# One reciprocal and one addition per pair of heads in an attention and two-expert kernel

## The chip, the cores and the metric

The kernel runs on one NeuronCore of a Trainium2 chip. The metric is the device time of one launch in microseconds. The engines are called TensorE (PE in the profile, its weight loads PEld), VectorE (DVE), ScalarE (ACT), POOL (GpSimd) and SyncE (SP); each takes its own instructions in order and waits for the others at semaphores.

## The reference

Inputs are q, k and v of shape 2 x 12 x 448 x 64 (batch, heads, positions, width) and two pairs of weights (768 x 2048 and 2048 x 768), all float32.

```python
scores = scale * np.matmul(q, k.transpose(0, 1, 3, 2))
scores = np.where(mask, -1000000000.0, scores)          # causal
scores = scores - np.max(scores, axis=-1, keepdims=True)
attn = np.exp(scores)
attn = attn / (np.sum(attn, axis=-1, keepdims=True) + 1e-09)
x = np.matmul(attn, v)                                  # then (896, 768)
h = x @ w_in                                            # first expert layer
x = (h * np.clip(h + 3.0, 0.0, 6.0) / 6.0) @ w_out
h = x @ w_in2                                           # second: P, Q from h, h^2, h^3
out = (P / (Q + 1e-06)) @ w_out2
```

The sum over a row of `attn` is what the change is about: `1e-09` is added to it, the reciprocal is taken, and the row is multiplied by that.

## The kernel before, in words

Attention goes by pairs of heads: `n` = 0 to 11 is one of six pairs of heads in one of two batches. The 448 positions are cut into seven chunks of 64. A chunk `r` of queries of both heads lies in 128 partitions (64 for each head) and sees (r + 1) x 64 keys, so the seven rows of a pair are 64, 128, ... 448 wide. For each pair there are these steps:

- `scores` (L633, TensorE, two steps), into banks of PSUM.
- `max` (L647, VectorE): adds the mask, writes the row to a tile `e`, and its maximum to the column of that row in a small tile `stat`. A row's tile has two buffers (`EB`), so pair n + 2 writes where pair n was.
- `exp` (L654, ScalarE): in place, with the row's sum as a second result (a short instruction that reads the accumulator follows each).
- `bias` (`a_bias`, L666): adds 1e-9 to the sums, on POOL for pairs 1 to 9, else on ScalarE or VectorE. `reciprocal` (`a_recip`, L670): on VectorE. Both are done twice in a pair: once for the columns of the straight rows 6, 5 and 0 (448, 384 and 64 wide), once for those of the swapped rows 4, 3, 2 and 1 (320, 256, 192 and 128 wide).
- `norm` (`a_norm`, L678): multiplies a row by its reciprocal, seven times in a pair. POOL does it for pairs 1 to 9; for pairs 0, 10 and 11 VectorE and ScalarE may, too.
- `transpose` (L686, TensorE): 14 small transposes for the straight rows, 14 for the swapped ones, each group into two banks.
- `move` (L508, L510): those four banks into SBUF, by ScalarE or VectorE.
- `apply` (L708, TensorE): times v; `x hi` and `x rest` split the result into two parts (L508 and L720).

The order is not written by hand. Every step is added with its cost, the engines that may do it and a due time, and `Program.order` plays the engines in a model of time: again and again it takes, of the steps that can begin, the one that can begin earliest; steps that lie within `LOOK` of an engine's earliest count as equally early, and of these the one with the lowest due time is taken. `AVERSE` is a charge in us on a step for an engine, `STAY` one on the due time where TensorE would change its tiling mode (scores, transposes, apply and the products have different ones). The due time is the pair's time plus entries of `DUE`, `SHIFT`, `HURRY` and `FINE`. The order that results is what each engine's queue gets; on the chip, semaphores alone decide when an instruction begins. Loads of q, k and v are DMAs issued by SyncE, among the weights' loads.

The two expert stages are products (`product`, L940): 2304 matmuls with three passes for each tile of weights and batch. Weights come in chunks of three tiles, in float64, and are split into two float32 parts by ScalarE and VectorE (`top` L846, `join` L851, `w hi` L508, `w rest` L869). The first products may begin, pair by pair, once all scores are done, so that they stand among the last pairs' transposes and applies.

Of the kernel before, what the change touches and what calls it, by code (L numbers as in the profile page):

```python
# [21 lines left out]
NCH = 7  # L22
# [19 lines left out]
class Program:  # L42
# [15 lines left out]

    TILING = {"scores": "quarters", "transpose": "rows", "apply": "columns"}
    DRAIN = 0.16  # L60
    STAY = 142.07
    LOOK = {"act": 0.025, "dma": 0.000, "dve": 0.061, "pe": 0.143, "pool": 0.000}
    UNTIL = 90.0
    AVERSE = {("bias", "act"): 23.796, ("bias", "dve"): 0.010, ("move", "act"): 0.010, ("move", "dve"): 0.028, ("norm", "act"): 9.289, ("w hi", "act"): 0.220, ("w hi", "pool"): 0.908}

    def __init__(self, rings, banks, due):
        self.rings, self.banks, self.due = rings, banks, due
# [159 lines left out]
def c_mm(n, passes):  # L227
# [2 lines left out]


DUE = {
    "load": 641.06,
    "keep": 0.00,
    "fetch": -20.00,
    "load v": 986.54,
    "norm": 605.40,
    "scores": -621.59,
    "max": 453.18,
    "exp": 669.50,  # L240
    "bias": -555.36,
    "reciprocal": -3821.56,
    "transpose": -2284.96,
    "move": -1862.28,
    "apply": -251.47,
    "x hi": -335.61,
    "x rest": -1522.19,
    "constants": 166.20,
    "w load": 1207.86,
    "top": 1391.57,  # L250
    "join": 4152.81,
    "w hi": 3197.25,
    "w rest": 1692.49,
    "product": 0.00,
    "relu": -472.26,
    "gate": -35.40,
# [18 lines left out]
    "store": 7.50,  # L275
}
PAIR = 5.5
SHIFT = {0: -402.17, 1: 59.39, 2: -1243.06, 3: -600.07, 4: -53.66, 5: -852.91, 6: -483.55, 7: -206.83, 8: -52.38, 9: 238.94, 10: 591.04, 11: 134.07}

HURRY = {0: 1406.07, 1: -2185.22, 2: -1459.89, 3: -470.07, 4: -843.76, 5: -462.43, 6: 966.12, 7: -966.25, 8: -1410.93, 9: 889.14, 10: -1126.45, 11: -161.36}  # L280
FINE = {
    ("apply", 0): -900.09,
    ("apply", 1): -361.68,
    ("apply", 2): 713.65,
    ("apply", 3): -51.47,
    ("apply", 4): 56.64,
    ("apply", 5): -605.77,
    ("apply", 6): -213.06,
    ("apply", 7): -760.02,
    ("apply", 8): 961.00,  # L290
    ("apply", 9): -43.05,
    ("apply", 10): 335.21,
    ("apply", 11): -376.05,
    ("bias", 0): 226.99,
    ("bias", 1): -289.77,
    ("bias", 2): -1211.59,
    ("bias", 3): -661.92,
    ("bias", 4): 137.09,
    ("bias", 5): 909.85,
    ("bias", 6): -84.77,  # L300
    ("bias", 7): 31.83,
    ("bias", 8): 194.45,
    ("bias", 9): -548.16,
    ("bias", 10): 1678.18,
    ("bias", 11): 960.60,
    ("exp", 0): -272.24,
    ("exp", 1): 296.63,
    ("exp", 2): 1968.38,
    ("exp", 3): 135.65,
    ("exp", 4): 1497.08,  # L310
    ("exp", 5): -310.31,
    ("exp", 6): -1124.12,
    ("exp", 7): 123.92,
    ("exp", 8): -625.90,
    ("exp", 9): -93.28,
    ("exp", 10): -1001.23,
    ("exp", 11): 388.45,
    ("load", 0): -1063.61,
    ("load", 1): -1277.69,
    ("load", 2): 140.13,  # L320
    ("load", 3): 251.36,
    ("load", 4): 146.42,
    ("load", 5): -37.97,
    ("load", 6): 782.51,
    ("load", 7): -328.43,
    ("load", 8): 554.29,
    ("load", 9): -193.50,
    ("load", 10): -67.48,
    ("load", 11): 512.54,
    ("load v", 0): -77.97,  # L330
    ("load v", 1): 587.48,
    ("load v", 2): 124.45,
    ("load v", 3): 878.92,
    ("load v", 4): -626.75,
    ("load v", 5): -695.84,
    ("load v", 6): 341.59,
    ("load v", 7): 545.32,
    ("load v", 8): 832.41,
    ("load v", 9): -802.78,
    ("load v", 10): 327.34,  # L340
    ("load v", 11): -114.21,
    ("max", 0): 162.46,
    ("max", 1): 780.96,
    ("max", 2): 324.74,
    ("max", 3): 559.50,
    ("max", 4): 694.16,
    ("max", 5): -572.65,
    ("max", 6): 553.74,
    ("max", 7): 296.32,
    ("max", 8): -353.83,  # L350
    ("max", 9): -428.08,
    ("max", 10): 1388.07,
    ("max", 11): 403.46,
    ("move", 0): 1230.75,
    ("move", 1): 1212.60,
    ("move", 2): -1400.97,
    ("move", 3): 1123.55,
    ("move", 4): 8.69,
    ("move", 5): 686.35,
    ("move", 6): -202.87,  # L360
    ("move", 7): 296.53,
    ("move", 8): 881.18,
    ("move", 9): 1710.46,
    ("move", 10): 172.45,
    ("move", 11): -165.14,
    ("norm", 0): 402.44,
    ("norm", 1): -274.51,
    ("norm", 2): -1317.40,
    ("norm", 3): 1224.05,
    ("norm", 4): -405.04,  # L370
    ("norm", 5): -119.22,
    ("norm", 6): -950.02,
    ("norm", 7): -460.55,
    ("norm", 8): -406.99,
    ("norm", 9): 532.31,
    ("norm", 10): 985.93,
    ("norm", 11): 850.79,
    ("reciprocal", 0): 132.61,
    ("reciprocal", 1): -682.70,
    ("reciprocal", 2): 476.82,  # L380
    ("reciprocal", 3): -497.26,
    ("reciprocal", 4): 215.96,
    ("reciprocal", 5): -308.28,
    ("reciprocal", 6): 510.69,
    ("reciprocal", 7): -798.76,
    ("reciprocal", 8): -500.60,
    ("reciprocal", 9): 254.09,
    ("reciprocal", 10): 427.19,
    ("reciprocal", 11): -262.09,
    ("scores", 0): 1319.98,  # L390
    ("scores", 1): 44.03,
    ("scores", 2): -675.00,
    ("scores", 3): 317.05,
    ("scores", 4): 1376.15,
    ("scores", 5): 741.99,
    ("scores", 6): 436.50,
    ("scores", 7): 701.37,
    ("scores", 8): -1737.51,
    ("scores", 9): -134.48,
    ("scores", 10): 606.54,  # L400
    ("scores", 11): -305.58,
    ("transpose", 0): -673.78,
    ("transpose", 1): -1595.48,
    ("transpose", 2): -282.36,
    ("transpose", 3): -614.95,
    ("transpose", 4): -257.88,
    ("transpose", 5): -1165.44,
    ("transpose", 6): -235.67,
    ("transpose", 7): -1067.59,
    ("transpose", 8): 344.74,  # L410
    ("transpose", 9): -54.30,
    ("transpose", 10): 521.17,
    ("transpose", 11): -740.95,
    ("x hi", 0): -623.98,
    ("x hi", 1): -1662.06,
    ("x hi", 2): 73.95,
    ("x hi", 3): -1809.87,
    ("x hi", 4): -10.52,
    ("x hi", 5): 376.53,
    ("x hi", 6): 8.43,  # L420
    ("x hi", 7): 16.98,
    ("x hi", 8): 357.94,
    ("x hi", 9): -975.33,
    ("x hi", 10): 98.15,
    ("x hi", 11): -867.64,
    ("x rest", 0): -707.65,
    ("x rest", 1): 396.94,
    ("x rest", 2): 1345.13,
    ("x rest", 3): 838.55,
    ("x rest", 4): 400.60,  # L430
    ("x rest", 5): 291.33,
    ("x rest", 6): 419.34,
    ("x rest", 7): -416.87,
    ("x rest", 8): -292.29,
    ("x rest", 9): -598.63,
    ("x rest", 10): -252.52,
    ("x rest", 11): -615.30,
}


# [18 lines left out]
def tile_attention_moe_moe2(  # L459
# [134 lines left out]
    STRAIGHT, SWAPPED = (6, 5, 0), (4, 3, 2, 1)  # L594
# [44 lines left out]
    LINEUP = [r for held in (STRAIGHT, SWAPPED) for r in held]  # L639
# [16 lines left out]
            accum_out=stat[:, 1, at_:at_ + 1],  # L656
        )

    PARTS = slice(0, len(STRAIGHT)), slice(len(STRAIGHT), NCH)

    def a_bias(e, n, part):
        stat, c = tiles["stat", n], PARTS[part]
# [62 lines left out]
    def put(kind, at, *what, **uses):  # L725
        add(kind, at + FINE.get((kind, n), 0.0), *what, **uses)

    for n in range(len(pairs)):
        t, last = PAIR * n + SHIFT.get(n, 0.0), n == len(pairs) - 1
        b, hp = pairs[n]  # L730
        for which in ("kr", "qr"):

            group, whole = (which, "all", hp), hp > 1
            if whole and b:
                continue
            for parts in ((0,), (1,)) if n == 0 else ((0, 1),):
# [5 lines left out]
                    writes=[(which, x, j) for x in range(n, n + (B if whole else 1)) for j in parts],  # L742
                    new=[(which, group)] if b == 0 and 0 in parts else (),
                )
        if b == 0:
            put(
                "load v", t, {"dma": 4.3}, v_load, hp, reads=[("empty", hp % VB)],
                writes=[("v", hp), ("turn", "v")], new=[("v", ("v", hp))],
            )
        for step in range(2):  # L750
# [3 lines left out]
                reads=[(w, *x) for w in ("kr", "qr") for x in ((n, 0), (n, 1), ("all", hp))],  # L754
                writes=sc + [("turn", "scores")] + ["scored"] * last, new=[("s", key) for key in sc],
            )
        for late, r in enumerate(order if n else (1, 3, 5, 4, 6, 2, 0)):
            w, first, mine = (r + 1) * CP, late == 0, next(h for step in steps(n) for h in step if r in h)
# [10 lines left out]
            )  # L769
        t += HURRY.get(n, 0.0)  # L770
        for part, held in list(enumerate((STRAIGHT, SWAPPED)))[::1 if n else -1]:
            put(
                "bias", t + 2 * part, {"pool": 0.2} if 0 < n < 10 else {"act": 0.2, "dve": 0.1}, a_bias, n, part,
                reads=[("st", n, r) for r in held] + [("stat", n)], writes=[("r", n, part)],
            )
            put(
                "reciprocal", t + 2 * part, {"dve": 0.15}, a_recip, n, part, reads=[("stat", n)],
                writes=[("r", n, part)],
            )
            for r in held:  # L780
                w = (r + 1) * CP
                put(
                    "norm", t + 2 * part, c_norm(n, r, w), a_norm, n, r,
                    reads=[("r", n, part), ("stat", n)], writes=[("e", n, r)],
                )
        for g, held in list(enumerate((STRAIGHT, SWAPPED)))[::1 if n else -1]:
            pt = [("pt", n, g, slot) for slot in range(2)]
# [393 lines left out]
```

## Time and profile before

| | |
|---|---|
| time, median of 3 runs | 535.29 us (535.19 to 537.04) |
| profiled execution | 537.02 us |
| its span, first to last instruction | 535.2 us |
| TensorE busy | 527.4 us (99%) |
| VectorE, ScalarE, POOL busy | 359.4, 338.1, 48.2 us |
| mean granted TensorE clock | 0.997 |

The page's forty slices (each a fortieth of the span) show the attention stage as the part in which POOL works:

```
PE   7999999999999999999999999999999999999997
DVE  5798976787878755645543099988888888843310
ACT  5999956577768655555543188767776777645210
POOL 4676630000000000000000000000000000000000
PEclk9899999999999999999999999999999999999999
```

A digit is the busy share in tenths, 9 for 90% or more; PEclk is the granted clock. Busy times of TensorE come from modelled ends, so a 9 is not proof that it runs at its peak; idle time before an instruction is proof that it waited.

### The profile page before, as it was taken

Reading aid. Unit: us, or ns where it says so; the run is one execution under the profiler, and the core shown is the slowest. Engines: PE = TensorE matmul, PEld = TensorE weight load, DVE = VectorE, ACT = ScalarE, POOL = GpSimd, SP = SyncE. Lnnn points to the kernel's source line nnn. Section 1 sums busy time; section 2 is a strip of 40 time slices with the busy share of each in tenths; the row PEclk is TensorE's granted clock in tenths of the full one; section 3 lists DMA queues with packets and bytes.
Section 4 is the critical chain, followed back from the end, with each engine's and each line's share of the span. In section 5 each row is a group of like instructions: output and inputs, shape, how many; then the busy total and the mean of one; then the engine's idle time right before and its main releaser. Section 6 shows DMA issues by size and latency. Waiting matters only on the chain.

```text
span 535.2 us, 9589 instructions
## 1 busy us (share of the span) xinstructions
PE 527.4 (99%) x3472; PEld 485.3 (91%) x3472; DVE 359.4 (67%) x801; ACT 338.1 (63%) x737; POOL 48.2 (9%) x113
## 2 busy tenths in 40 slices
PE   7999999999999999999999999999999999999997
PEld 6787889999999999999999999999999999999996
DVE  5798976787878755645543099988888888843310
ACT  5999956577768655555543188767776777645210
POOL 4676630000000000000000000000000000000000
PEclk9899999999999999999999999999999999999999
DMA  6778453587777787877774332433443244246000
GB/s 167 184 192 257 126 177 91 157 295 262 258 264 269 234 290 242 292 250 259 258 265 148 118 108 70 148 90 94 136 124 90 90 127 136 62 140 213 21 36 34
DMA packets 42512, 90.64 MB, mean 169 GB/s; under 512 B 4833, under 2 KB 17121, under 8 KB 42465
## 3 DMA queue, kind: packets, MB, share of 16 engines
q1 hardware_dynamic: 42304, 89.81, 53.0%
q8 instruction: 27, 0.44, 0.3%
q10 hardware_dynamic: 160, 0.23, 0.1%
q14 instruction: 21, 0.16, 0.1%
HBM read 73.50 MB, written 16.52 MB: 168 GB/s over the span
## 4 chain that ended last, share of the span: by engine, by line
PE 96%; DVE 1%; POOL 1%; DMA 1%; issue 0%; ACT 0%; SPq 0%; POOLq 0%; DVEq 0%
PE bank L940 86%; PE bank L708 4%; PE bank L633 3%; PE bank L686 2%; POOL e L678 1%; DMA qr<-in_qT 1%; DVE e L647 1%; DVE et L510 0%; POOL stat L666 0%; SPq L583 0%; ACT et L508 0%; ACT o L508 0%; DVE xl L720 0%; DVE stat L670 0%; DVE e L678 0%
## 5 line engine op out<-in xcount | busy, mean ns | idle before, releaser
L846 ACT ACTIVATE top<-raw 128x384 f16<-128x384 bf16 x128 | 77.8, 639 | 59.5 <-DVE full L851 46.9
L940 PE MATMUL bank<-yh,w 128*128 128x448 f32 x384 | 112.2, 362 | 0.0
L940 PE MATMUL bank<-rh,w 128*128 128x448 f32 x384 | 97.0, 362 | 0.0
L869 DVE TENSOR_TENSOR w<-full,w 128x384 fp32r<-128x384 f32 x93 | 51.6, 556 | 66.3 <-ACT w L508 66.0
L940 PE MATMUL bank<-xh,w 128*128 128x448 f32 x384 | 93.8, 364 | 0.0
L940 PE MATMUL bank<-ph,w 128*128 128x448 f32 x384 | 92.6, 362 | 0.0
L508 ACT ACTIVATE w<-full 128x384 fp32r<-128x384 f32 x90 | 47.0, 523 | 60.5 <-PE bank L940 60.5
L940 PEld LDWEIGHTS bank<-yh,w 128*128 128x128 f32 x384 | 72.0, 188 | 5.0
L940 PEld LDWEIGHTS bank<-rh,w 128*128 128x128 f32 x384 | 71.9, 187 | 5.0
L940 PEld LDWEIGHTS bank<-ph,w 128*128 128x128 f32 x384 | 72.0, 188 | 4.6
L940 PEld LDWEIGHTS bank<-xh,w 128*128 128x128 f32 x384 | 71.6, 188 | 4.8
L851 DVE SCALAR_TENSOR_TENSOR full<-raw,top 128x384 uint32<-128x384 uint32 x128 | 68.7, 559 | 1.3 <-ACT top L846 0.3
L940 PE MATMUL bank<-yl,w 128*128 128x448 f32 x192 | 69.4, 361 | 0.0
L940 PE MATMUL bank<-rl,w 128*128 128x448 f32 x192 | 54.6, 362 | 0.0
L940 PE MATMUL bank<-xl,w 128*128 128x448 f32 x192 | 53.8, 361 | 0.0
L940 PE MATMUL bank<-pl,w 128*128 128x448 f32 x192 | 53.7, 361 | 0.0
L654 ACT ACTIVATE e<-e,stat 128x448 f32<-128x448 f32 (+6 forms) x84 | 41.7, 502 | 5.6 <-DVE stat L647 5.3
L678 POOL TENSOR_SCALAR e<-e,stat 128x256 f32<-128x256 f32 (+6 forms) x77 | 37.4, 504 | 15.4 <-DVE stat L670 11.5
L940 PEld LDWEIGHTS bank<-xl,w 128*128 128x128 f32 x192 | 36.0, 187 | 2.7
L940 PEld LDWEIGHTS bank<-pl,w 128*128 128x128 f32 x192 | 36.0, 187 | 2.6
L940 PEld LDWEIGHTS bank<-rl,w 128*128 128x128 f32 x192 | 36.0, 188 | 2.4
L940 PEld LDWEIGHTS bank<-yl,w 128*128 128x128 f32 x192 | 36.0, 187 | 2.3
(58 smaller groups left out, 626.7 us busy)
## 6 DMA issues: line engine op xcount, KB each, us to landing
raw<-in_w SPq DMA_DIRECT2D x128, 383.8 KB, 3.8
kept<-ws SPq DMA_DIRECT2D x35, 384.0 KB, 3.4
w<-kept SPq DMA_DIRECT2D x35, 384.0 KB, 3.4
out_T<-o SPq DMA_DIRECT2D x12, 224.0 KB, 2.0
kr<-in_kT SPq DMA_DIRECT2D x8, 224.0 KB, 3.6
qr<-in_qT SPq DMA_DIRECT2D x8, 224.0 KB, 4.2
v<-in_v SPq DMA_DIRECT2D x12, 128.0 KB, 4.0
v<-in_v SPq DMA_DIRECT2D x12, 96.0 KB, 3.7
```

The costliest lines, as they stand in the source:

```text
L508: e.activation(out, in_, AF.Copy)
L633: e.matmul(tiles["sc", n, r][halves[slot], done:done + hi - lo], q[halves[j], r * CP:w], k[halves[j], lo:hi], start=True, stop=True,)
L647: e.tensor_tensor_reduce(e_tile(n, r), tiles.pop(("sc", n, r)), over, -0.125, 3.0e38, ALU.add, ALU.min, tiles["stat", n][:, 0, at_:at_ + 1],)
L654: e.activation(t, t, AF.Exp, bias=stat[:, 0, at_:at_ + 1], scale=-1.0, accum_out=stat[:, 1, at_:at_ + 1],)
L678: e.tensor_scalar(t, t, by, 1.0, ALU.mult, ALU.mult)
L686: e.transpose(pt[slot][:, x * CP:(x + 1) * CP], block(n, what)[rows], ident[rows, rows])
L708: e.matmul(o[halves[j], r * CP:(r + count) * CP], vt[:, c, halves[j]], et[slot][:, x * CP:(x + count) * CP], start=g == 0 and m == 0, stop ...
L846: e.activation(out, raw[i].bitcast(BF16)[:, :, :, 2], AF.Copy)
L851: e.scalar_tensor_tensor(full[i].bitcast(U32), bits, 13, top.pop(i), ALU.logical_shift_right, ALU.bitwise_or)
L869: e.tensor_tensor(split[i][:, 1], full.pop(i), split[i][:, 0], ALU.subtract)
L940: e.matmul(sums[which, m, b], split[i][:, w, j, :], x, start=k == 0 and n == 0, stop=last and n == 2,)
```

## The change

For pairs 1 to 11 `a_bias` and `a_recip` are called once for all seven columns (a third entry of `PARTS`), and every normalisation of the pair depends on that one reciprocal, which depends on all seven exponentials. Pair 0 keeps its two parts. All due times up to the weights' are new, as are `STAY`, `LOOK` and `AVERSE`; those of the expert stages' own steps are as before.

```diff
-    STAY = 142.07
-    LOOK = {"act": 0.025, "dma": 0.000, "dve": 0.061, "pe": 0.143, "pool": 0.000}
+    STAY = 169.49
+    LOOK = {"act": 0.029, "dma": 0.000, "dve": 0.175, "pe": 0.328, "pool": 0.179}
...
-    AVERSE = {("bias", "act"): 23.796, ("bias", "dve"): 0.010, ("move", "act"): 0.010, ("move", "dve"): 0.028, ("norm", "act"): 9.289, ("w hi", "act"): 0.220, ("w hi", "pool"): 0.908}
+    AVERSE = {("bias", "act"): 26.763, ("bias", "dve"): 0.070, ("norm", "act"): 8.162, ("norm", "dve"): 8.443, ("norm", "pool"): 0.148, ("w hi", "act"): 0.874, ("w hi", "pool"): 0.927}
...
-    "norm": 605.40,
-    "scores": -621.59,
+    "norm": -243.99,
+    "scores": -82.12,
...
-    "bias": -555.36,
-    "reciprocal": -3821.56,
-    "transpose": -2284.96,
+    "bias": -1038.72,
+    "reciprocal": -3558.38,
+    "transpose": -2595.47,
...
-    "top": 1391.57,
-    "join": 4152.81,
-    "w hi": 3197.25,
-    "w rest": 1692.49,
+    "top": 1146.99,
+    "join": 4421.49,
+    "w hi": 4518.47,
+    "w rest": 2257.95,
...
-    PARTS = slice(0, len(STRAIGHT)), slice(len(STRAIGHT), NCH)
+    PARTS = slice(0, len(STRAIGHT)), slice(len(STRAIGHT), NCH), slice(0, NCH)
...
         for part, held in list(enumerate((STRAIGHT, SWAPPED)))[::1 if n else -1]:
-            put(
-                "bias", t + 2 * part, {"pool": 0.2} if 0 < n < 10 else {"act": 0.2, "dve": 0.1}, a_bias, n, part,
-                reads=[("st", n, r) for r in held] + [("stat", n)], writes=[("r", n, part)],
-            )
-            put(
-                "reciprocal", t + 2 * part, {"dve": 0.15}, a_recip, n, part, reads=[("stat", n)],
-                writes=[("r", n, part)],
-            )
+            whole = part == 0 and n
+            if part == 0 or not n:
+                which = 2 if whole else part
+                put(
+                    "bias", t + 2 * part, {"pool": 0.2} if 0 < n < 10 else {"act": 0.2, "dve": 0.1}, a_bias,
+                    n, which, reads=[("st", n, r) for r in (LINEUP if whole else held)] + [("stat", n)],
+                    writes=[("r", n, which)],
+                )
+                put(
+                    "reciprocal", t + 2 * part, {"dve": 0.15}, a_recip, n, which, reads=[("stat", n)],
+                    writes=[("r", n, which)],
+                )
             for r in held:
                 w = (r + 1) * CP
                 put(
                     "norm", t + 2 * part, c_norm(n, r, w), a_norm, n, r,
-                    reads=[("r", n, part), ("stat", n)], writes=[("e", n, r)],
+                    reads=[("r", n, which), ("stat", n)], writes=[("e", n, r)],
                 )
```

## Rows read from the trace of the kernel before

**Rows 1.** The page's chain of waits, shares of the span by engine and line.
```profile
PE bank L940 86%; PE bank L708 4%; PE bank L633 3%; PE bank L686 2%; POOL e L678 1%; DMA qr<-in_qT 1%; DVE e L647 1%; DVE et L510 0%; POOL stat L666 0%; SPq L583 0%; ACT et L508 0%; ACT o L508 0%; DVE xl L720 0%; DVE stat L670 0%; DVE e L678 0%
```
**Rows 2.** Stretches: their length, then us busy of each engine, granted clock, DMA share.
```profile
10.00:20.00 10.00, 7.61 (x125) 5.84 (x120) 7.65 (x42) 8.89 (x33) 6.09 (x14) 0.83 0.71 182
20.00:30.00 10.00, 9.48 (x193) 7.91 (x188) 8.28 (x35) 9.40 (x33) 7.45 (x19) 1.00 0.80 200
30.00:40.00 10.00, 10.00 (x196) 8.12 (x194) 9.17 (x42) 10.00 (x37) 7.19 (x18) 1.00 0.69 179
40.00:50.00 10.00, 9.78 (x188) 7.76 (x188) 7.62 (x30) 9.19 (x32) 7.17 (x17) 1.00 0.82 233
50.00:60.00 10.00, 10.00 (x200) 8.04 (x196) 9.54 (x40) 9.94 (x35) 6.26 (x15) 1.00 0.68 198
```
**Rows 3.** The chain in order of time: start, duration in us, what.
```profile
24.01 0.23 POOL stat L666
24.24 0.09 issue
24.33 2.32 POOL e L678 x5
...
76.68 455.09 PE bank L940 x2274
```
**Rows 4.** Timeline of TensorE: start, us, what, in brackets idle before and its releaser.
```profile
13.44 1.59 PE L686 MATMUL bank<-ident,e 64*128 64x64 f32 x28 [2.39 <-DVE e L678]
14.96 2.10 PE L633 MATMUL bank<-kr,qr 64*64 64x384 f32 x16
...
26.69 1.29 PE L686 MATMUL bank<-ident,e 64*128 64x64 f32 x28 [0.44 <-POOL e L678]
...
30.55 1.08 PE L633 MATMUL bank<-kr,qr 64*64 64x448 f32 x16
31.56 0.65 PE L686 MATMUL bank<-ident,e 64*128 64x64 f32 x14
...
55.26 0.65 PE L686 MATMUL bank<-ident,e 64*128 64x64 f32 x14
...
68.34 1.09 PE L686 MATMUL bank<-ident,e 64*128 64x64 f32 x28
```
**Rows 5.** Stretches, as in the second group, of one us.
```profile
14.00:15.00 1.00, 1.00 (x21) 0.88 (x18) 0.65 (x2) 0.55 (x1) 0.92 (x3) 0.50 0.52 146
```
**Rows 6.** Lines L666 and L670: duration in ns min/median/max, first and last start.
```profile
L666 POOL TENSOR_SCALAR stat<-stat x18: 223/235/358, 12.6 to 59.6; 128x3 f32<-128x3 f32 x9, 128x4 f32<-128x4 f32 x9
...
L666 DVE TENSOR_SCALAR stat<-stat x6: 138/160/472, 10.7 to 68.9; 128x3 f32<-128x3 f32 x3, 128x4 f32<-128x4 f32 x3
...
L670 DVE RECIPROCAL stat<-stat x24: 158/175/180, 10.9 to 69.7; 128x3 f32<-128x3 f32 x12, 128x4 f32<-128x4 f32 x12
```
**Rows 7.** Groups of normalisations: busy us, mean ns, idle before them.
```profile
L678 POOL TENSOR_SCALAR e<-e,stat 128x448 f32<-128x448 f32 x12 | 8.1, 672 | 9.4 <-DVE stat L670 9.4
L678 POOL TENSOR_SCALAR e<-e,stat 128x384 f32<-128x384 f32 x11 | 6.5, 595 | 0.1
L678 POOL TENSOR_SCALAR e<-e,stat 128x64 f32<-128x64 f32 x9 | 2.9, 319 | 0.3
...
L678 POOL TENSOR_SCALAR e<-e,stat 128x256 f32<-128x256 f32 (+6 forms) x77 | 37.4, 504 | 15.4 <-DVE stat L670 11.5 <-DVE stat L647 2.0 <-DVE stat L666 1.0
...
L678 DVE TENSOR_SCALAR e<-e,stat 128x64 f32<-128x64 f32 (+4 forms) x7 | 2.5, 373 | 0.0
```
**Rows 8.** Timeline of POOL and ScalarE: start, us, what, idle before.
```profile
11.22 1.25 POOL L678 TENSOR_SCALAR e<-e,stat 128x448 f32<-128x448 f32 x2 [5.95 <-DVE stat L670]
13.76 0.19 ACT L654 ACTIVATION_READ_ACCUMULATOR e<-e,stat 128x1 f32 x1
15.16 2.21 POOL L678 TENSOR_SCALAR e<-e,stat 128x64 f32<-128x64 f32 x5
...
32.72 0.22 POOL L666 TENSOR_SCALAR stat<-stat 128x4 f32<-128x4 f32 x1 [1.45 <-ACT e L654]
...
53.17 1.74 POOL L678 TENSOR_SCALAR e<-e,stat 128x320 f32<-128x320 f32 x4 [0.51 <-DVE stat L670]
```

More of the change, by code (lines that the diff above doesn't have):

```diff
@@ L232 @@
 DUE = {
-    "load": 641.06,
+    "load": 238.47,
     "keep": 0.00,
     "fetch": -20.00,
-    "load v": 986.54,
-    "norm": 605.40,
-    "scores": -621.59,
-    "max": 453.18,
-    "exp": 669.50,
-    "bias": -555.36,
-    "reciprocal": -3821.56,
-    "transpose": -2284.96,
[L244 to L247, printed above, removed]
-    "constants": 166.20,
-    "w load": 1207.86,
-    "top": 1391.57,
-    "join": 4152.81,
-    "w hi": 3197.25,
-    "w rest": 1692.49,
+    "load v": 581.27,
+    "norm": -243.99,
+    "scores": -82.12,
+    "max": 393.91,
+    "exp": 584.45,
+    "bias": -1038.72,
+    "reciprocal": -3558.38,
+    "transpose": -2595.47,
+    "move": -2143.17,
+    "apply": -651.94,
+    "x hi": -270.26,
+    "x rest": -1687.32,
+    "constants": 166.20,
+    "w load": 1758.70,
+    "top": 1146.99,
+    "join": 4421.49,
+    "w hi": 4518.47,
+    "w rest": 2257.95,
     "product": 0.00,
@@ L277 @@
 PAIR = 5.5
-SHIFT = {0: -402.17, 1: 59.39, 2: -1243.06, 3: -600.07, 4: -53.66, 5: -852.91, 6: -483.55, 7: -206.83, 8: -52.38, 9: 238.94, 10: 591.04, 11: 134.07}
-HURRY = {0: 1406.07, 1: -2185.22, 2: -1459.89, 3: -470.07, 4: -843.76, 5: -462.43, 6: 966.12, 7: -966.25, 8: -1410.93, 9: 889.14, 10: -1126.45, 11: -161.36}
+SHIFT = {0: -423.93, 1: -20.41, 2: -1176.93, 3: -759.35, 4: -281.41, 5: -839.96, 6: -708.25, 7: -360.12, 8: -292.69, 9: 146.83, 10: 961.27, 11: 46.28}
+HURRY = {0: 935.94, 1: -4036.28, 2: -2815.46, 3: -1198.17, 4: -1583.75, 5: -1450.15, 6: 1074.06, 7: -2710.09, 8: -1794.86, 9: 1609.78, 10: -929.99, 11: 56.06}
@@ L281 @@
 FINE = {
[L282 to L437, printed above, removed]
+    ("apply", 0): -373.28,
+    ("apply", 1): -619.25,
+    ("apply", 2): 407.50,
+    ("apply", 3): -285.05,
+    ("apply", 4): -304.38,
+    ("apply", 5): -842.36,
+    ("apply", 6): -416.08,
+    ("apply", 7): -831.32,
@@ new lines @@
+    ("apply", 8): 1061.40,
+    ("apply", 9): 249.32,
+    ("apply", 10): 447.11,
+    ("apply", 11): -489.00,
+    ("bias", 0): -385.90,
+    ("bias", 1): -656.47,
+    ("bias", 2): -1022.68,
+    ("bias", 3): -941.39,
+    ("bias", 4): 9.83,
+    ("bias", 5): 1209.96,
+    ("bias", 6): -388.48,
+    ("bias", 7): -522.54,
+    ("bias", 8): 171.49,
+    ("bias", 9): -701.32,
+    ("bias", 10): 1482.58,
+    ("bias", 11): 819.58,
+    ("exp", 0): -683.87,
+    ("exp", 1): 627.02,
+    ("exp", 2): 2032.82,
@@ new lines @@
+    ("exp", 3): 240.86,
+    ("exp", 4): 1269.28,
+    ("exp", 5): -172.17,
+    ("exp", 6): -1325.89,
+    ("exp", 7): -8.18,
+    ("exp", 8): -239.38,
+    ("exp", 9): 302.18,
+    ("exp", 10): -982.91,
+    ("exp", 11): 467.12,
+    ("load", 0): -1301.35,
+    ("load", 1): -1587.79,
+    ("load", 2): -313.96,
+    ("load", 3): 26.54,
+    ("load", 4): 308.01,
+    ("load", 5): 310.45,
+    ("load", 6): 844.81,
+    ("load", 7): -306.20,
+    ("load", 8): 567.97,
+    ("load", 9): -153.10,
+    ("load", 10): -22.65,
@@ new lines @@
+    ("load", 11): 444.69,
+    ("load v", 0): 24.53,
+    ("load v", 1): 814.77,
+    ("load v", 2): -144.63,
+    ("load v", 3): 937.37,
+    ("load v", 4): -271.40,
+    ("load v", 5): -1119.39,
+    ("load v", 6): 89.49,
+    ("load v", 7): 420.55,
+    ("load v", 8): 1126.45,
+    ("load v", 9): -370.25,
+    ("load v", 10): 45.54,
+    ("load v", 11): 439.29,
+    ("max", 0): 519.78,
+    ("max", 1): 564.36,
+    ("max", 2): 584.30,
+    ("max", 3): 395.46,
+    ("max", 4): 400.38,
+    ("max", 5): -595.22,
@@ new lines @@
+    ("max", 6): 584.38,
+    ("max", 7): 162.32,
+    ("max", 8): -533.70,
+    ("max", 9): 221.83,
+    ("max", 10): 1499.51,
+    ("max", 11): 411.77,
+    ("move", 0): 1702.07,
+    ("move", 1): 985.56,
+    ("move", 2): -1942.96,
+    ("move", 3): 1682.11,
+    ("move", 4): 466.86,
+    ("move", 5): 722.12,
+    ("move", 6): -260.45,
+    ("move", 7): 11.10,
+    ("move", 8): 934.73,
+    ("move", 9): 1843.57,
+    ("move", 10): 94.41,
+    ("move", 11): 64.39,
+    ("norm", 0): 666.96,
+    ("norm", 1): -493.45,
@@ new lines @@
+    ("norm", 2): -1440.89,
+    ("norm", 3): 1080.49,
+    ("norm", 4): -200.68,
+    ("norm", 5): -303.46,
+    ("norm", 6): -1024.22,
+    ("norm", 7): -815.99,
+    ("norm", 8): -574.46,
+    ("norm", 9): 628.41,
+    ("norm", 10): 1123.94,
+    ("norm", 11): 1224.30,
+    ("reciprocal", 0): 406.31,
+    ("reciprocal", 1): -549.32,
+    ("reciprocal", 2): 23.61,
+    ("reciprocal", 3): -895.77,
+    ("reciprocal", 4): 630.17,
+    ("reciprocal", 5): -207.72,
+    ("reciprocal", 6): 629.32,
+    ("reciprocal", 7): -1353.77,
@@ new lines @@
+    ("reciprocal", 8): -557.58,
+    ("reciprocal", 9): 515.13,
+    ("reciprocal", 10): 412.48,
+    ("reciprocal", 11): -296.16,
+    ("scores", 0): 795.37,
+    ("scores", 1): 125.06,
+    ("scores", 2): -640.09,
+    ("scores", 3): -73.08,
+    ("scores", 4): 1315.31,
+    ("scores", 5): 692.14,
+    ("scores", 6): 453.31,
+    ("scores", 7): 151.75,
+    ("scores", 8): -1560.36,
+    ("scores", 9): -75.68,
+    ("scores", 10): 505.41,
+    ("scores", 11): -573.14,
+    ("transpose", 0): -365.91,
@@ new lines @@
+    ("transpose", 1): -1523.51,
+    ("transpose", 2): -599.12,
+    ("transpose", 3): -469.03,
+    ("transpose", 4): -787.85,
+    ("transpose", 5): -1076.84,
+    ("transpose", 6): -100.36,
+    ("transpose", 7): -1207.71,
+    ("transpose", 8): 599.23,
+    ("transpose", 9): 39.84,
+    ("transpose", 10): 818.71,
+    ("transpose", 11): -474.16,
+    ("x hi", 0): -343.70,
+    ("x hi", 1): -2017.01,
+    ("x hi", 2): 505.86,
+    ("x hi", 3): -1808.62,
+    ("x hi", 4): 118.23,
+    ("x hi", 5): 494.60,
@@ new lines @@
+    ("x hi", 6): -153.25,
+    ("x hi", 7): 79.69,
+    ("x hi", 8): 233.62,
+    ("x hi", 9): -906.22,
+    ("x hi", 10): 197.41,
+    ("x hi", 11): -503.90,
+    ("x rest", 0): -625.52,
+    ("x rest", 1): 654.44,
+    ("x rest", 2): 1290.14,
+    ("x rest", 3): 1017.86,
+    ("x rest", 4): 362.48,
+    ("x rest", 5): 268.35,
+    ("x rest", 6): 750.87,
+    ("x rest", 7): -593.50,
+    ("x rest", 8): -171.84,
+    ("x rest", 9): -263.00,
+    ("x rest", 10): -307.61,
+    ("x rest", 11): -724.13,
```

## The prediction, made before the changed kernel was run

> **What bounds the kernel now.** I read the chain of waits first. Of the span it gives 86% to TensorE's products in the two expert stages (L940) and 4, 3 and 2% to its apply (L708), scores (L633) and transposes (L686) of the attention stage; no line of another engine has more than 1% [rows 1]. So only two things can move the time: the work that TensorE has to do, which the change leaves alone, and the time that it does not work. The table of stretches shows where that is: TensorE is busy 7.61 of 10 us from 10 to 20, 9.48 from 20 to 30, 9.78 from 40 to 50, and all of 30 to 40 and 50 to 60 [rows 2]. Idle in these fifty us: 2.39 + 0.52 + 0.22 = 3.1 us. From 76.68 the products run as one piece of 455.09 us [rows 3]; there is nothing to be had behind it, and the code of that stage is the same but for the due times of the weights.
>
> The other columns of the same table matter as much: ScalarE is busy 89 to 100% and VectorE 76 to 95% in these stretches, POOL 61 to 75% [rows 2]. So POOL and VectorE, whose instructions the change removes, are not the engines that are full. ScalarE, which has the exponentials, is nearly as full as TensorE and gets nothing.
>
> TensorE's timeline then says what its lost time is. Before the first transposes (13.44) it sat idle for 2.39 us, and a clock granted at 0.50, the 1.2 GHz level, followed [rows 4, 5]. In that stretch 28 transposes took 1.59 us where a later 28 took 1.09, and 16 score matmuls took 2.10 where a later 16 took 1.08 [rows 4]: 0.50 + 1.02 = 1.5 us for the low clock. At 26.69 it waited 0.44 us for a normalisation on POOL [rows 4]. Each change between scores, transposes and apply also costs a little: two separate groups of 14 transposes take 2 x 0.65 = 1.30 us against 1.09 for 28 in one go [rows 4], 0.2 us.
>
> **What goes.** Pair 0 keeps its two parts. Pairs 1 to 11 each lose one addition and one reciprocal. Eleven reciprocals of 0.175 us are 1.9 us of VectorE; nine additions of 0.235 us are 2.1 us of POOL (pairs 1 to 9), and two of 0.160 us are 0.3 us of VectorE [rows 6]. That the one that stays has seven columns instead of three or four should cost next to nothing: the medians are taken over both widths and the smallest to largest reciprocal lie between 158 and 180 ns; I allow 0 to 0.02 us each, 0.2 us in all, off the path. The removed 4.3 us lie on two engines with idle time, beside TensorE's work, and are worth nothing where TensorE is full. One place is on the chain: from 24.01 POOL does an addition (0.23 us), then after 0.09 us five normalisations to 26.65, and then TensorE starts [rows 3]. Without that addition POOL is 0.32 us earlier, and the 0.44 us of idle time shrink by as much. Bounds: 0, if the wait for later exponentials takes its place, to -0.44 us. I take **-0.3 us**.
>
> **What is added: a wait.** The normalisations of rows 6, 5 and 0 of a pair (448, 384 and 64 wide) now wait for all seven exponentials, not for their three. Their means on POOL are 672, 595 and 319 ns, together 1.59 us [rows 7]; all seven take 7 x 0.504 = 3.5 us. For pair 1 the last exponential is finished at 13.95 [rows 8]; with addition (0.235), reciprocal (0.175) and three hand-overs (0.09 each, as between 24.24 and 24.33) its normalisations can begin at 14.6 and end by 18.1, where its last five now end at 17.4 [rows 8]. Behind the waiting instruction on POOL stand the next pair's addition and normalisations only, and behind those the transposes. In the middle pairs the price is at most 1.59 - 0.24 = 1.35 us of delay for a pair's last normalisation, in those pairs where POOL is now done with the first three before the last exponential comes. Such a pair is seen at 32.72, where POOL idled 1.45 us for ScalarE [rows 8]. In the others POOL works straight through and the delay is less, down to -0.3 us. TensorE can cover it by doing scores or apply of another pair first; in the full stretches it never lacked such work [rows 2]. I take **0** for the forecast, and keep the other end for a rival.
>
> **What is moved.** Every due time is new, so the order of all engines is worked out afresh. One edit can be read without that order: a charge of 8.4 us now stands on a normalisation by VectorE. The seven that VectorE does today (2.5 us, pairs 0, 10 and 11) [rows 7] will go to POOL. For pairs 10 and 11 products fill TensorE's gaps, so this costs nothing there. For pair 0 it is the opening. POOL begins at 11.22 [rows 8]; if the group of three comes first it is ready at 11.22 + 1.59 = 12.8, and TensorE starts there rather than at 13.44: -0.6 us. Bounds: -0.9 us, if TensorE takes the straight group as soon as today's two wide ones are done (12.47, [rows 8]); +1.3 us, if it waits for all seven on POOL, 11.22 + 3.5 = 14.7. I take **-0.6 us**, since the due time of the three lies 2 us before that of the four. The low clock I leave as it is.
>
> That low clock has a page. The Trainium skill ("TensorE: Matmul & The Clock Gate", Part 1) calls the slow state the default that only activity lifts, and says that the same kernel can meet the ramp differently from run to run. The row here shows one drop, behind the 2.39 us gap. By the page 1.5 us could go or stay without the change having a part in it; by the row the gap is the cause, and a shorter one might not bring it.
>
> The weights' preparation gets new due times and charges (the upper half is put later). Its cover is that the chunks are ready ahead of TensorE, which runs the 455 us without a gap; so nothing can be gained there. I take 0, and at most +1.2 us where one chunk's tile is late, the time of six matmuls of 0.20 us (455.09 / 2274, [rows 3]).
>
> **Sum.** -0.3 - 0.6 = -0.9 us. The profiled execution took 537.02 us with a span of 535.2, so 1.8 us lie around it; its span would become 534.3. The runs shown have a median of 535.29, near the span alone, so I forecast 535.29 - 0.9 = **534.4 us**. About 0.5%, 2.7 us, is what can be told from no change here, so this counts as within it.
>
> **Rivals.**
> - *The opening closes.* The gap falls short enough that the clock stays at 2.4 GHz (-1.5 us), and groups that become ready together are transposed in one go in four pairs (4 x 0.2 = -0.8 us). With -0.9: 532.1 us. For it: a pair's seven rows are now ready together, and the planner's charge for a change of mode rises from 142 to 169. Against it: the gap remains near 1.8 us by my own sum.
> - *The long hold* (slower). A pair's probability tiles have two buffers. They are held from the first maximum to the last transpose; if the hold grows by 1.35 us, the maxima two pairs on wait, then their banks, then TensorE's scores. Transposes follow closely already: four normalisations from 53.17 end at 54.91, and TensorE takes them at 55.26 [rows 4, 8], 0.35 us of room. So 1.0 us is paid at each turn of the ring, four turns in pairs 2 to 9: +4 us, 539.3 us. It decides from where the delay exceeds that room and no scores or apply of another pair is ready. For it: ScalarE at 92 to 100%, so lost exponential time is not made good. Against it: POOL and VectorE have idle time of their own (POOL 2.5 to 3.9 us in ten, [rows 2]) and lose 4.3 us of work, and in the middle pairs the first three are seldom done long before the last exponential.
> - *Nothing.* The removed instructions were never in the way and the opening is the same: 535.3 us. For it: 4.3 us of work off the path. Against it: the two places at 13.4 and 26.7 wait for just these engines.
> - *The planner decides, not the merge:* with all due times new, the opening waits for seven normalisations on POOL, +1.3 us and the same clock: 536.6 us.
>
> **Chances.** Forecast 0.40, nothing 0.13, the planner's later opening 0.09, the opening closes 0.20, the long hold 0.18. The first three stay within half a per cent (532.6 to 538.0) but for some 0.02, put half on each side. That makes faster 0.21, within 0.5% 0.60, slower 0.19. The range leaves about a tenth on either side: from 531.2 (the opening closes, and the rest of its 0.9 us bound and three more merged groups come with it) to 539.2 (the full price of the ring).
>
> **What would show it.** Right: one addition and one reciprocal per pair from pair 1 on (13 and 13 in all), POOL's normalisations 84; TensorE's first transposes near 12.8; no idle at 26.7; no new idle on TensorE between 30 and 60; the first piece of pure products starting near 75.8. Wrong: TensorE idle between 20 and 60 above 1 us behind POOL (the long hold), a granted clock without a drop, or a start of the first transposes after 13.44. If the long piece of products has a gap, I missed the weights.

## The result and the profile after

The changed kernel takes 539.04 us (median; 538.97 to 539.41), the kernel before 535.94 beside it (535.19 to 537.04). The ratio is 1.0052 (95% interval 1.0035 to 1.0069): half a per cent slower, where 534.4 us was forecast. The profiled execution took 538.97 us with a span of 537.2. The kernel before has runs near 535.4 and runs near 536.8; its profiled one is of the second group, the four runs of the changed kernel were alike.

What was to be done was done: 13 additions (9 on POOL, 4 on VectorE), 13 reciprocals, 84 normalisations, all on POOL. Lines L666, L670 and L678 of the changed kernel, as in [rows 6]:

```profile
L666 POOL TENSOR_SCALAR stat<-stat x9: 242/243/254, 13.4 to 59.9; 128x7 f32<-128x7 f32 x9
...
L666 DVE TENSOR_SCALAR stat<-stat x4: 165/170/254, 9.6 to 69.7; 128x7 f32<-128x7 f32 x2, 128x4 f32<-128x4 f32 x1, 128x3 f32<-128x3 f32 x1
...
L670 DVE RECIPROCAL stat<-stat x13: 177/197/205, 9.8 to 69.8; 128x7 f32<-128x7 f32 x11, 128x4 f32<-128x4 f32 x1, 128x3 f32<-128x3 f32 x1
...
L678 POOL TENSOR_SCALAR e<-e,stat x84: 308/481/970, 10.2 to 74.0; 128x320 f32<-128x320 f32 x12, 128x448 f32<-128x448 f32 x12, 128x384 f32<-128x384 f32 x12, 128x64 f32<-128x64 f32 x12
```

A reciprocal of seven columns takes 0.197 us where one of three or four took 0.175, an addition 0.243 for 0.235.

The stretches of the changed kernel, columns as in [rows 2]:

```profile
10.00:20.00 10.00, 7.33 (x123) 5.66 (x117) 5.96 (x31) 7.98 (x29) 6.67 (x15) 0.83 0.67 176
20.00:30.00 10.00, 10.00 (x196) 8.05 (x195) 7.63 (x33) 9.36 (x34) 6.53 (x16) 1.00 0.90 217
30.00:40.00 10.00, 9.48 (x175) 7.36 (x169) 7.62 (x34) 9.29 (x31) 5.75 (x14) 1.00 0.69 173
40.00:50.00 10.00, 10.00 (x192) 7.76 (x189) 8.25 (x35) 9.84 (x36) 6.44 (x16) 1.00 0.81 228
50.00:60.00 10.00, 10.00 (x190) 7.87 (x188) 9.38 (x35) 9.72 (x34) 6.53 (x15) 1.00 0.74 227
```

TensorE's idle time in these fifty us is 2.67 + 0.52 = 3.2 us, where it was 3.1: no long wait came. Yet the last piece of products starts at 78.36, not 76.68 [rows 3]. The chain in order of time (start, us, what):

```profile
76.44 1.92 PE bank L708 x36
78.36 273.01 PE bank L944 x1364
351.38 0.01 issue
351.39 182.31 PE bank L944 x910
```

So 1.7 us are lost ahead of it by a TensorE that is busy, and 0.3 us more behind.

The two profiles also differ in something that is not the change's. In that of the kernel before, TensorE's first scores are slow. Its weight loads and its matmuls of 384 columns between 5.5 and 6.5 us (count, then us busy, mean ns), first the kernel before, then the changed one:

```profile
L633 PEld LDWEIGHTS bank<-kr,qr 64*64 64x64 f32 x11 | 1.2, 223 | 0.1
L633 PE MATMUL bank<-kr,qr 64*64 64x384 f32 x4 | 1.5, 872 | 0.0
...
L633 PEld LDWEIGHTS bank<-kr,qr 64*64 64x64 f32 x16 | 1.0, 133 | 0.2
L633 PE MATMUL bank<-kr,qr 64*64 64x384 f32 x4 | 0.9, 508 | 0.0
```

The granted clock is 1.00 in both there. VectorE's second maximum waits for these scores, and what follows in the opening is 0.6 to 0.8 us late:

```profile
6.87 0.43 DVE L647 CUSTOM_DVE_ANT_0 e<-bank,mask 128x256 f32<-128x256 f32 x1 [0.52 <-PE bank L633]
...
6.25 0.42 DVE L647 CUSTOM_DVE_ANT_0 e<-bank,mask 128x256 f32<-128x256 f32 x1
```

Of the fourteen profiles of this case seven have the second maximum at 6.66 to 7.02 and seven at 6.10 to 6.31, and either kind occurs with either opening. What decides it is not shown. So a start of 13.44 before and of 13.39 after does not say that the opening is as good as it was: starts have to be compared within one kind.

Where TensorE's busy time grew, one pair of the middle shows. TensorE's timeline, first the kernel before from one apply to the next:

```profile
48.37 1.99 PE L708 MATMUL bank<-et,v 128*64 128x128 f32 x36
50.29 0.65 PE L686 MATMUL bank<-ident,e 64*128 64x64 f32 x14
50.87 1.96 PE L633 MATMUL bank<-kr,qr 64*64 64x448 f32 x32
52.76 0.65 PE L686 MATMUL bank<-ident,e 64*128 64x64 f32 x14
53.34 1.99 PE L708 MATMUL bank<-et,v 128*64 128x128 f32 x36
```

and the changed kernel, with its opening and its one new wait in front:

```profile
13.39 1.09 PE L686 MATMUL bank<-ident,e 64*128 64x64 f32 x28 [2.48 <-POOL e L678]
14.67 2.14 PE L633 MATMUL bank<-kr,qr 64*64 64x384 f32 x16 [0.19 <-ACT et L508]
...
31.54 0.65 PE L686 MATMUL bank<-ident,e 64*128 64x64 f32 x13 [0.52 <-DVE xl L720]
...
48.78 1.99 PE L708 MATMUL bank<-et,v 128*64 128x128 f32 x36
50.70 0.65 PE L686 MATMUL bank<-ident,e 64*128 64x64 f32 x14
51.29 1.08 PE L633 MATMUL bank<-kr,qr 64*64 64x448 f32 x16
52.30 0.65 PE L686 MATMUL bank<-ident,e 64*128 64x64 f32 x14
52.88 1.16 PE L633 MATMUL bank<-kr,qr 64*64 64x384 f32 x16
53.96 1.99 PE L708 MATMUL bank<-et,v 128*64 128x128 f32 x36
```

The same work takes 53.34 - 48.37 = 4.97 us before and 53.96 - 48.78 = 5.18 after. The two score steps that stood together (1.96) now stand on either side of the second group of transposes (1.08 + 1.16). Ahead of the last piece of products the kernel before has 49 stretches of one kind of work on TensorE, the changed one 56. Taking each stretch from its start to the start of the next, without idle time, scores take 25.5 us where they took 24.4, transposes 14.3 and 14.2, apply 23.2 and 23.1, the products in between 7.0 and 6.8.

Three theories were tested. **A**: the loss is TensorE's changes of mode, of which its new order has more. **B**: the wait for seven exponentials holds the probability tiles longer (the prediction's rival). **C**: the opening, with seven normalisations of pair 0 on POOL, starts later and meets the low clock more often.

### The profile page after: what moved, and what is told of

It is laid out like the page before. It is cut to its first block, busy times and chain, and to the rows that moved or that the text cites. A ratio compares the mean times of both kernels' runs of the same rounds, so it can differ in the third digit from the quotient of the medians.

```text
span 537.2 us, 9568 instructions
## 1 busy us (share of the span) xinstructions
PE 529.0 (98%) x3472; PEld 484.9 (90%) x3472; DVE 357.6 (67%) x779; ACT 340.5 (63%) x738; POOL 49.0 (9%) x112
## 4 chain that ended last, share of the span: by engine, by line
PE 96%; DVE 1%; ACT 1%; DMA 1%; POOL 1%; issue 0%; SPq 0%; ACTq 0%
PE bank L944 86%; PE bank L708 4%; PE bank L633 3%; PE bank L686 2%; DVE e L647 1%; DMA qr<-in_qT 1%; POOL e L678 1%; ACT e L654 1%; ACT et L508 0%; DVE xl L720 0%; DVE et L510 0%; SPq L583 0%; ACT o L508 0%; ACT xh L508 0%; DVE stat L666 0%
## 5 line engine op out<-in xcount | busy, mean ns | idle before, releaser
L508 ACT ACTIVATE w<-full 128x384 fp32r<-128x384 f32 x89 | 45.8, 516 | 35.0 <-PE bank L944 34.7
L678 POOL TENSOR_SCALAR e<-e,stat 128x320 f32<-128x320 f32 (+6 forms) x84 | 40.5, 504 | 11.2 <-DVE stat L666 4.9
```

The source lines that it names most:

```text
L508: e.activation(out, in_, AF.Copy)
L678: e.tensor_scalar(t, t, by, 1.0, ALU.mult, ALU.mult)
```

## The experiments

All ratios are to the kernel before, run on the same chip in turn, with 95% intervals.

**The score steps put together again.** Behind the planner, in the changed kernel:

```diff
-        for (_, _, _, fn, args, _, _, _), e, banks in self.order():
+        for (_, _, _, fn, args, _, _, _), e, banks in join(self.order()):
```

`join` moves the second score step ahead of the transposes (or these behind it) where no step between them touches the same banks or data.

> The changed kernel, with one thing more: where the two score steps of pairs stand on either side of a group of transposes in TensorE's queue, they are put together (8 changes of mode fewer before the last product piece: 48 stretches of one mode instead of 56, the kernel before has 49). Merge, waits and all other queues as in the change. Theory A (changes of mode, some 0.2 us each, are what the change costs): 1.3 to 1.8 us less than the 539.0 us of the change, so about 537.4, score time of TensorE back from 25.5 to 24.4 us. Theory B (the wait for all seven exponentials holds buffers longer): no gain, 538.7 to 539.5.

545.02 us, 1.0165 (1.0148 to 1.0182): 6 us slower than the change. It has 48 stretches instead of 56, but TensorE now waits. The rows of its timeline that show idle time of 0.4 us or more behind the first scores:

```profile
13.99 1.76 PE L733 MATMUL bank<-ident,e 64*128 64x64 f32 x28 [2.88 <-POOL e L725]
...
28.90 0.65 PE L733 MATMUL bank<-ident,e 64*128 64x64 f32 x14 [0.81 <-DVE et L557]
...
34.15 1.46 PE L680 MATMUL bank<-kr,qr 64*64 64x384 f32 x16 [1.01 <-ACT et L555]
...
57.05 1.37 PE L680 MATMUL bank<-kr,qr 64*64 64x384 f32 x16 [0.43 <-DMA raw<-in_w]
```

The moves (`et`) give the banks back too late for a score step or a group of transposes that comes early. So the price of the order can't be had back by this reordering: the changes of mode stand where nothing else was ready. The run says nothing on their price.

**The merge in a part of the pairs, due times of before.** The merge of all eleven pairs under the old due times, and the new due times without the merge, were not run. In the kernel before, the change's edit with this difference merges from pair 4 on (a second run: from pair 5 on):

```diff
-            whole = part == 0 and n
-            if part == 0 or not n:
+            both = n >= 4
+            whole = part == 0 and both
+            if part == 0 or not both:
```

> The kernel before, due times and all, with the merge in pairs 4 to 11 alone (8 of the 11). Its planned TensorE order has 50 stretches of one mode, one more than the kernel before. Theory A: 0 to +0.4 us against the kernel before. Theory B: 8/11 of the loss of about 2 us, +1.5 us or more.

544.87 us, 1.0162 (1.0145 to 1.0180). Neither theory had this. Its TensorE waits 0.98, 2.42 and 0.68 us for POOL and VectorE between 68 and 74 us, and the granted clock is 0.66 from 70 to 80 us: an order that was good in the planner's model of time and not on the chip. It decides nothing on A or B.

> The kernel before, its due times, with the merge in pairs 5 to 11 alone (7 of 11). Its planned TensorE order has 54 stretches of one mode, five more than before, and shows the order of the change (transposes, scores, transposes, scores, apply) in pairs 5 to 9. Theory A: +0.8 to +1.2 us against the kernel before, more than the run with eight merged pairs. Theory B: 7/11 of the loss, +1.3 us, and less than the run with eight merged pairs. That the new due times make the order: no such pattern, +0.

536.53 us, 1.0010 (1.0000 to 1.0021): 0.8 us above the median of the kernel before. Ten of its eleven runs kept their clock (0.999 or 1.000); against the runs of the kernel before with a clock of 1.000 beside it (median 535.45) it is 1.1 us. The pattern transposes, scores, transposes, scores, apply is there in the middle pairs under the old due times, so it comes with the merge. Five more stretches for 0.8 to 1.1 us agree with A, but B's 1.3 is too near to be ruled out by this run.

**Changes of mode alone.** In the kernel before, ahead of a score step that follows another (`BROKEN` holds the six such places behind the opening):

```diff
+        if (n, step) in BROKEN:
+            e.transpose(bank[banks[0]][:, :CP], still[halves[0], :], ident[halves[0], halves[0]])
```

> The kernel before, without the merge, with one small transpose (64 rows of zeros, overwritten at once) put between two adjoining score steps at the six places behind the opening where two stand together: 12 changes of mode more, nothing else. Theory A: +1.2 to +2.4 us (0.1 to 0.2 a change and six matmuls of some 0.03). Theory B: the six matmuls alone, +0.2 us.

538.81 us, 1.0040 (1.0025 to 1.0055). Its runs fall into the two groups of the kernel before, near 537.5 and 538.9, each 2.1 us above (535.4 and 536.8). One of the six places in its timeline:

```profile
52.16 1.08 PE L643 MATMUL bank<-kr,qr 64*64 64x448 f32 x16
53.17 0.27 PE L631 MATMUL bank<-ident,still 64*128 64x64 f32 x1
53.38 1.16 PE L643 MATMUL bank<-kr,qr 64*64 64x384 f32 x16
```

1.08, then a single matmul of 0.21 us from start to start, then 1.16, for the 1.96 of two steps together. 2.1 us / 12 changes = 0.17 us a change, the six matmuls included. A's price is shown; seven changes are 1.2 us.

**The change again, and its opening undone.**

> The changed kernel as it is, run many times beside the kernel before, whose 18 runs fall into two groups, near 535.4 (10) and near 536.8 (8). Theory C (the changed opening, with seven normalisations of pair 0 on POOL, always meets the low clock; the kernel before meets it in some runs alone): all runs of the change in one group, 538.9 to 539.5. If the change costs the same in every run: two groups as before, near 537.6 and 539.0.

539.29 us, 1.0061 (1.0046 to 1.0077); six runs, none near 537.6. C had one group from 538.9 to 539.5. Four runs lie from 538.7 to 539.6, one of them with a clock of 1.000 (538.68), and two at 540.6 with 0.994: not the two groups of before, and not one group either.

For the opening undone, in `play`:

```diff
+            if kind == "norm" and args[0] == 0 and args[1] in (0, 4, 2, 1):
+                e = "dve"
```

> The changed kernel with one thing undone: the four narrower normalisations of pair 0 (rows 4, 2, 1 and 0) go to VectorE again, as in the kernel before, at the same places of the order; nothing else. Theory C: first transposes near 12.6 instead of 13.4 (-0.8 us), and the gap before them short enough that the clock stays at 2.4 GHz in most runs (-1.4 us): 536.7 to 537.2 us in most runs, 1 to 1.5 us above the kernel before, which the changes of mode leave. Theory A alone (changes of mode are all of it): 539.0 us, as the change.

538.76 us, 1.0048 (1.0034 to 1.0062): 0.5 us less than the change, with intervals that overlap, and not 2.2. The first transposes of the profiled run, one with slow first scores, start at 13.25 behind a gap of 2.27 us, and the clock falls all the same. C was too large.

**The gap filled.** Nine matmuls of zeros (seven for the kernel before) ahead of the first transposes:

```diff
+        if not filled:
+            for _ in range(9):
+                e.matmul(pt[0][:, :P], still, still, start=True, stop=True)
+            filled.append(n)
```

> The changed kernel with nine matmuls of zeros (128 x 128) on TensorE in the gap before its first transposes, into a bank that these overwrite; nothing else. They take some 2.0 of the 2.5 us. Theory C: the granted clock stays at 1.00 from 5 to 60 us and the time falls by the 1.4 to 1.5 us of the low clock, to 537.5. If the low clock costs nothing, because another engine is late anyway: 539.0.

> The kernel before with seven such matmuls of zeros (some 1.6 us) before its first transposes. Theory C: the group of runs near 536.8 goes away, all runs lie at 535.0 to 535.9, and the median is some 0.3 us lower. If the two groups have another cause than the clock: two groups as now.

538.30 us, 1.0039 (1.0027 to 1.0051), 1.0 us less than the change beside it; and 535.51 us, 0.9990 (0.9982 to 0.9999), eleven runs from 535.1 to 536.0 and no second group. The granted clock is 1.00 in both. So the kernel before has its second group from the low clock in the opening: filled, it is 0.1% faster than the median of both groups, and no faster than the first. In the opening of the kernel before, filled:

```profile
10.90 1.83 PE L686 MATMUL bank<-still 128*128 128x128 f32 x14
12.72 1.14 PE L692 MATMUL bank<-ident,e 64*128 64x64 f32 x28
```

Its transposes start at 12.72, those of the changed kernel, filled, at 14.10. Half of these 1.4 us is not the change's: this execution has slow first scores (second maximum at 6.95, not 6.27). Within one kind, the change starts at 13.39 and the opening of the kernel before at 12.66 (merged from pair 5):

```profile
12.66 1.14 PE L686 MATMUL bank<-ident,e 64*128 64x64 f32 x28 [1.76 <-DVE e L678]
```

So 0.7 us is the opening on POOL.

**The work that was removed, put back.** Two additions and two reciprocals behind one another at the place of one:

```diff
+        if part == 2:
+            a_bias(e, n, 0)
+            a_bias(e, n, 1)
+            return
```

(and the same in `a_recip`)

> The changed kernel, its order and its one wait for all seven exponentials, but at the place of each pair's one addition and one reciprocal two of each stand behind one another (three and four columns): the work that the change removed is back, and nothing else. If the removed 4 us of POOL and VectorE are off the path: 538.9 to 539.6, as the change. If that work was worth something: up to +1 us.

539.17 us, 1.0059 (1.0042 to 1.0077), as the change (539.04 and 539.29). The removed work was worth nothing that these runs can tell. This profiled run kept its clock behind a gap as long as the change's; TensorE's first transposes and the stretch around them, with the granted clock third from the end:

```profile
13.48 1.09 PE L694 MATMUL bank<-ident,e 64*128 64x64 f32 x28 [2.41 <-POOL e L686]
```

```profile
10.00:20.00 10.00, 7.41 (x151) 5.94 (x147) 6.86 (x35) 9.14 (x31) 7.17 (x17) 1.00 0.66 171
```

The change's own row has 0.83 there. Yet the span is 536.9, only 0.3 us less than the change's: the scores of pair 4 now wait. TensorE comes to them at 21.96 instead of 23.25, and they take 2.59 us instead of 1.80. Weight loads of TensorE in that run:

```profile
21.96 0.19 PEld L633 LDWEIGHTS bank<-kr,qr 64*64 64x64 f32 x2
22.72 1.59 PEld L633 LDWEIGHTS bank<-kr,qr 64*64 64x64 f32 x30 [0.58 <-issue]
```

In the trace the second half of that pair's q lands at 22.62. In the change's own trace it landed at 21.18, and TensorE, with the low clock, came at 23.25. So in this execution 0.8 of the 1.3 us that the clock gave back went into the wait for a DMA. With q landing at 21.18 there would have been no wait; the filled runs had a shorter one at the same place (0.5 us, q at 21.85 and 22.04).

**The opening alone, in the kernel before.** The edit that undid the opening, here with `e = "pool"` and for all seven rows:

> The kernel before with the change's opening alone: all seven normalisations of pair 0 on POOL. Theory C: first transposes 0.8 to 1.3 us later, a longer gap, the low clock in every run: one group of runs, 537.2 to 538.0, +1.5 to +2.2 us against the median of before. If the opening is not what the change loses: 535.4 and 536.8 in two groups, as before.

538.22 us, 1.0039 (1.0026 to 1.0052), +1.7 us; one of the nine runs took 1350.46 us, for a reason that is not known, and without it the median is 538.1. TensorE's first transposes come at 14.62, and the clock stays low twice as long (until 20):

```profile
14.62 1.75 PE L688 MATMUL bank<-ident,e 64*128 64x64 f32 x28 [3.60 <-POOL e L680]
```

The edit costs what C says in this order, where POOL takes the wide rows first and TensorE the narrow ones; in the change's own order POOL's is better, and undoing it gave 0.5.

**What is left behind the opening.** The change with its opening undone and filled by seven matmuls:

> The changed kernel with pair 0's opening undone and the gap filled with seven matmuls of zeros, so that its opening is that of the kernel before filled (535.5). What is left is the order behind it. Theory A: seven changes of mode more (some 1.4 us) and the wait of 0.5 us near 31.4 in place of two of 0.44 and 0.22: +1.3 to +1.8 us, 536.9 to 537.3. If the order costs nothing: 535.5.

538.38 us, 1.0040 (1.0025 to 1.0056), against 0.9990 for the kernel before filled: 0.5%, 2.7 us, more than expected. The spans are 536.1 and 533.3. Of the 2.8 us between them 2.3 lie ahead of the last piece of products: taken as above, scores 25.5 for 23.7, transposes 13.9 for 13.8, products 7.0 for 6.8, idle and filling together equal within 0.2. 0.3 us of the scores is a first step after the opening of 1.5 us instead of 1.2; the rest, some 2 us, lies in seven more stretches. By the price above these are 1.2 us; what the other 0.8 is, no run divides. The other 0.5 us of the 2.8 lie among the products. Waits of TensorE's weight loads from 80 to 530 us, in this run:

```profile
PEld bank L952 <- DVE w L881: 0.4, 1, 0.4
PEld bank L952 <- DMA w<-kept: 0.2, 1, 0.2
```

The first stands in the changed kernel, too (at 351 us), and no such wait is in the kernel before: a chunk's second part comes late under the new due times.

**A third buffer.** The changed order with three buffers for a pair's probability tiles:

```diff
-        for x in range(EB)
+        for x in range(EB + 1)
...
-        return es[n % EB][t][:, at_:at_ + (r + 1) * CP]
+        return es[n % (EB + 1)][t][:, at_:at_ + (r + 1) * CP]
```

> The changed kernel with the same queues, but three buffers instead of two for a pair's probability tiles, so that no maximum waits for transposes of two pairs before. Theory B (the long hold): 1.5 to 3 us less, 536.3 to 537.7. Theories A and C: 538.7 to 539.4, at most 0.3 us less.

538.99 us, 1.0050 (1.0031 to 1.0068), within the change's. So B falls: on the chip nothing is lost by waiting for a tile of two pairs before. (The order itself was planned with two buffers.)

## Why the prediction was wrong

- *What bounds the kernel*: right. TensorE's lost time and its own work set the end. But I took its work as fixed, "which the change leaves alone", and read the price of changes of mode [rows 4] only as a gain to be had. That price of 0.2 us was also too high: it adds durations that overlap, and from start to start two groups of 14 take 1.2 us for the 1.0 of 28.
- *What goes*, -0.3 us: the idle 0.44 us at 26.7 did go (20 to 30 us is full now), and a wait of 0.52 us at 31.5 took its place, for VectorE's split of an earlier pair. That the rest is worth nothing was right, and shown by putting it back.
- *What is added*, taken as 0: **this is the step that failed.** I wrote that TensorE can cover the later normalisations by doing scores or apply of another pair first. It does, and that is the cost. Before, the two groups of a pair became ready far enough apart for a whole apply between them (pair 8: POOL's two blocks end at 52.3 and 54.9 and the apply of pair 7 stands from 53.34). Now they are ready one behind the other (55.4 and 57.4), too far apart to be one group and too close for an apply, and one score step goes between them. This reason is read from that pair; no run moved the two apart. One stretch more in such a pair costs 0.2 us; over all pairs the order of TensorE has 7 more, 1.2 us by the price of the split run, and some 2 us with what could not be divided.
- *What is moved*, -0.6 us: wrong in sign. All seven normalisations of pair 0 went to POOL as read. But TensorE still takes the swapped group first, and POOL's last one belongs to it: its seven run from 10.15 to 13.34, and the transposes start at 13.39. That is the prediction's own other end, a wait for all seven. And 13.44, from which the 0.6 us were to come off, was the start of an execution with slow first scores; with quick ones the opening of the kernel before starts at 12.66, 0.7 us ahead of the change's. The forecast then took the 0.6 us off 535.29, a time of the first group, of which no profile was kept. Undoing the opening brought back 0.5 us. The clock comes on top: that of all four timed runs of the change is below 1.00, while the kernel before keeps it in about half of its runs. Filling the gap brings back 1.0 us here and 0.3 us there.
- *The weights*, taken as 0, at most 1.2: 0.4 us, one late chunk.
- *The rivals*: the long hold had the time (539.3) for a wrong reason; its tiles weren't waited for. The later opening (+1.3) was a part of it. That the opening closes did not happen.
- *The low clock and the page*: I let the gap decide. The profiles show gaps of 2.27 and 2.42 us (the change again, the third buffer) with a fall of the clock behind them and one of 2.41 (two of each) without, in the same order of work; a gap of 1.76 us (merged from pair 5) had none. The Trainium skill ("TensorE: Matmul & The Clock Gate", Part 1) has it of the start of a kernel that one kernel can meet the ramp differently from run to run. The traces agree, with first weight loads of 223 ns in one execution and 133 in another, and show the same behind a gap.

In sum for the changed kernel, 3.1 us: the order of TensorE 1.2 to 2, the opening with its clock 0.6, the weights 0.4. The opening's 0.5 and its clock's 1.0 don't add up: undone together (539.29 to 538.38) they gave back 0.9, less the 0.3 that the kernel before loses by its clock. What stays open is how the 0.8 us beside the changes of mode divide; the due times of the weights alone were not tried, nor all the new due times without the merge.

## What to carry to other kernels

Where the bounding engine pays for changing its kind of work, count the stretches of one kind in its queue before and after; a wait that it "covers with other work" is not free when the other work is of another kind. Work taken from engines with idle time was worth nothing here by itself; what counted was what the new dependence did to the order of the full engine. And before two profiles are compared at one point, look whether the two executions are alike ahead of it.

## What the runs showed of the hardware that was not expected

- A single small transpose between two score steps costs 0.4 us, the two changes included (0.17 us a change over twelve).
- A gap of 2.3 to 2.5 us in TensorE's work was followed by a stretch at the 1.2 GHz level in most profiles and not in one; behind the 3.60 us of the opening on POOL that stretch was twice as long.
- TensorE's first scores took 1.7 times as long in some executions (weight loads of 223 ns, not 133) while the column of the granted clock showed 1.00.
- The clock's gain can go into a DMA: in one execution that kept 2.4 GHz, TensorE reached the next q 1.3 us earlier, and its scores took 0.8 us longer for a q that landed late.
